# Block attention and two MLPs on one core: y by column blocks at a unit's end, attention by pairs of groups

## The chip, the cores and the metric

One NeuronCore of a Trainium2 chip runs the whole program. The metric is the device time of one execution in microseconds; the lower the better. TensorE (PE) does the matrix products and the transposes, VectorE (DVE) and ScalarE (ACT) the elementwise work and the copies out of PSUM, GpSimd (POOL) elementwise work in SBUF only, and SyncE (SP) issues all DMAs.

## The reference, cut to what matters

```python
B, H, S, D = 2, 8, 768, 64;  block, window = 32, 16
k_sum = k.reshape(B, H, S // block, block, D).max(axis=3)
v_sum = v.reshape(B, H, S // block, block, D).mean(axis=3)
scores_l = q @ k.T / sqrt(D)        # kept where |i - j| < window
scores_s = q @ k_sum.T / sqrt(D) + log(block)
a = softmax(concat(masked scores_l, scores_s))
x = (a @ concat(v, v_sum)) -> rows are tokens: [1536, 512]
y = ((x @ w_a) * (x @ w_b)) @ w_out        # d_ff 1536
h = y @ w_in;  g = maximum(0.01 * h, h)    # d_ff 2048
out = g @ w_out2                           # [1536, 512]
```

All inputs are float32. The weights come in as 64-bit floats, seen as pairs of int32.

## The kernel before, in words

**Tokens and units.** The 1536 tokens are three blocks `c` of T = 512. In the first MLP the 12 slices `f` of 128 columns of `w_a` and `w_b` are taken in runs `s` of M1 = 4; one (s, c) is called a unit here, and there are nine. In the second MLP the 16 slices `f` are taken in runs of M2 = 8. A product of the MLPs is split into a high and a low part on both sides and costs three matmuls (`mm3`), so `x @ w_a` for one slice is 12 matmuls of 128x512. These are all on line 550: 864 for a and b, 432 for y, 576 and 576 in the second MLP, 2448 in all.

**First MLP.** For each slice the kernel writes out the product with `w_a` (bank "a"), the product with `w_b` (bank "b"), and then `y_acc` of the slice before: 12 matmuls that add to four PSUM banks c0 to c3, one for each 128 columns of y. At the unit's last slice the four banks are gathered into SBUF (`gather`). `b_out` multiplies a and b, and `parts` splits the result, in tiles of the pool "g" with two buffers.

**Weights.** A weight piece (512 KB) is loaded by `stage`, and `convert` makes float32 of it in seven steps: VectorE on lines 316, 324, 329, 335, 341 and 349, ScalarE on 320 and 346. The steps wait in the list `bg`. `tick` takes some from it at every `interleave` (three each), and `weights` takes whatever is still missing when a product wants its piece. Converted pieces live in W_EARLY = 15 slots, and in W_LATE = 9 more once the memory of the attention is given back (`att.close`).

**Attention.** A group is two heads by 256 tokens (`GT`), in four windows of 64; there are 24 groups, eight for each token block. `k_prep` transposes k and takes the block maxima, which line 455 copies beside each window. `q_prep` transposes q and writes it as a block-diagonal matrix `qbd` with four ScalarE copies, so that `scores` is four matmuls with the full 128x128 array (line 488; the trace counts two for each). VectorE adds the mask and takes the minimum (line 501), ScalarE takes the exponential (505), `normal` divides (513 and 514 on VectorE, the multiplication on GpSimd, line 515), `p_transpose` (523) and `pv` (534) follow; before `pv`, `put_sums` copies the block means beside the values (182, VectorE). The operations get positions, four to a group, and are written out in that order. Attention's PSUM banks are t0, t1, c2 and c3 during the first token block, and t0 and t1 after it.

**Order.** The first block's attention is written out first, with the products of slices 0 and 1 of block 0 (`early`). The attention of block c + 1 is spread over the products of unit (0, c), and what is left is written out at the unit's end. Instructions are then put in order by a list scheduler with a timeline of its own, by priority in the order written; an engine runs its instructions in the order that results.

Of the kernel before, what the change touches and what calls it, by code (L numbers as in the profile page):

```python
# [16 lines left out]
ALU = mybir.AluOpType  # L17
# [4 lines left out]
def kernel(  # L22
# [45 lines left out]
    W_EARLY, W_LATE = 15, 9  # L68
# [6 lines left out]
    acc_p = ctx.enter_context(tc.tile_pool(name="acc", bufs=2 * NE))  # L75
# [11 lines left out]
    at_banks = ["t0", "t1", "c2", "c3"]  # L87
# [9 lines left out]
    groups = []  # L97
    for c in range(NC):
        here = [divmod(c * GC + i, NGB) for i in range(GC)]
        if here[0][0] == here[-1][0]:  # L100
            groups.append([(b, hp, g) for hp in range(NP) for b, g in here])
        else:
            groups.append([(b, hp, g) for b, g in here for hp in range(NP)])
# [3 lines left out]
        keep.tile([P, NW + 1, SC], F32, tag=f"kts{i}", name=f"kts{i}") for i in range(NP)  # L107
    ]
    ks_t = [keep.tile([P, NB], F32, tag=f"ks{i}", name=f"ks{i}") for i in range(NP)]
    vw_t = [keep.tile([P, 2, G, D], F32, tag=f"vw{i}", name=f"vw{i}") for i in range(2)]  # L110
    qbd_t = [keep.tile([P, G, P], F32, tag=f"qbd{i}", name=f"qbd{i}") for i in range(2)]
# [7 lines left out]
    pace = {"micro": 0.0, "bg": 3}  # L119
# [10 lines left out]
    def load_q(b, hp, g):  # L130
        t = q_p.tile([P, 2, GT // P, D], F32, tag="q", name="q")
        nc.sync.dma_start(
            out=t,
            in_=q[b, 2 * hp : 2 * hp + 2, g * GT : (g + 1) * GT].rearrange(
                "c (p n) d -> p c n d", p=P
            ),
        )
        q_t[b, hp, g] = t
# [12 lines left out]
    def load_vw(b, hp, g):  # L151

        t = vw_t[cnt["load"] % 2]
        cnt["load"] += 1
# [15 lines left out]
        w0, w1 = int(g == 0), G - int(g == NGB - 1)  # L170
        if w0:
            rows(WIN, W, 0, 1)
        rows(0, W, w0, G)
        if w1 == G:
            rows(W, KL, 0, G)
        else:
            rows(W, W + WIN, 0, G)
            rows(W + WIN, KL, 0, w1)
        vw_of[b, hp, g] = t

    def put_sums(b, hp, g):
        nc.vector.tensor_copy(  # L182
            out=vw_of[b, hp, g][W : W + NB],
            in_=vs_t[b, 2 * hp // HV][:, 2 * hp % HV : 2 * hp % HV + 2, :]
            .unsqueeze(2)
            .to_broadcast([NB, 2, G, D]),
        )

    LOAD, SIDE, PRODUCT = range(3)
    PV = 9  # L190

    def attention_ops():

        ops = []
        seen = set()
        for i, x in enumerate(sum(groups, [])):
            b, hp, g = x
            n = 4 * i

            def add(at, kind, f, *args):  # L200
                ops.append((n + at, kind, lambda: f(*args), i))

            vi, r = divmod(2 * hp, HV)
            if (b, hp) not in seen:
                seen.add((b, hp))
                add(-11, LOAD, load_k, b, hp)
                for j in range(NGB):
                    add(j - 9, PRODUCT, k_prep, b, hp, j)
                if r == 0:
                    add(-1, LOAD, load_vb, b, vi)  # L210
                    add(-1, SIDE, v_sums, b, vi)
                    add(5, PRODUCT, v_place, b, vi)
# [9 lines left out]
        return ops  # L222

# [3 lines left out]
    for t in kts_t:  # L227
        nc.vector.memset(t[:, 0, 0:WIN], 0.0)
        nc.vector.memset(t[:, NW, WIN:KP], 0.0)
        nc.vector.memset(t[:, 0:NW, W + NB :], 0.0)  # L230
    for t in qbd_t:
        nc.vector.memset(t, 0.0)
# [29 lines left out]
    slices1 = [(s * M1 + i, c) for s in range(NF1 // M1) for c in range(NC) for i in range(M1)]  # L262
    slices2 = [(s * M2 + i, c) for s in range(NF2 // M2) for c in range(NC) for i in range(M2)]
    uses = [("a", 0), ("b", 0), ("a", 1), ("b", 1), ("a", 2), ("o", 0), ("b", 2), ("o", 1)]
    behind = ("o", 2)
    for f, c in slices1[3:]:
        uses += [("a", f), ("b", f), behind]
        behind = ("o", f)
    for f, c in slices2:
        uses += [("i", f), behind]  # L270
        behind = ("p", f)
    uses.append(behind)
# [87 lines left out]
    def tick(n):  # L360
        for _ in range(n):
            if not bg and may_convert():
                convert()
            if bg:
                bg.pop(0)()
# [3 lines left out]
    def weights(key):  # L369
# [3 lines left out]
        while key not in w_of:  # L373
            if not bg:
                convert()
            bg.pop(0)()
        w, home = w_of[key]
        if last_use[key] == i:
            room[home] += 1
        return w  # L380

# [54 lines left out]
    def k_prep(b, hp, g):  # L436
        k2 = k_t[b, hp]
        kts = kts_t[hp]
        ps = at_bank()
        for i in range(GT // P):  # L440
# [3 lines left out]
        src = ps[:, :GT].rearrange("p (w o) -> p w o", w=G)  # L444
        w0 = g * G
        nc.scalar.copy(out=kts[:, w0 : w0 + G, WIN:W], in_=src[:, :, 0 : W - WIN])
        nc.scalar.copy(out=kts[:, w0 + 1 : w0 + G + 1, 0:WIN], in_=src[:, :, W - WIN :])
        nc.vector.tensor_reduce(
            out=ks_t[hp][:, g * GT // BLK : (g + 1) * GT // BLK],
            in_=ps[:, :GT].rearrange("p (n j) -> p n j", j=BLK),  # L450
# [3 lines left out]
        if g == NGB - 1:  # L454
            nc.vector.tensor_copy(
# [6 lines left out]
    def q_prep(b, hp, g):  # L462
        q2 = q_t.pop((b, hp, g))
        i = cnt["q"] % 2
        cnt["q"] += 1
        qbd = qbd_t[i]
        ps = at_bank()
        for c in range(2):
            nc.tensor.transpose(
                ps[:, c * P : (c + 1) * P], q2[:, c].rearrange("p n d -> p (n d)"), ident  # L470
            )
        sc = -1.0 / math.sqrt(D)
        for c in range(2):

            dst = qbd[c * D : (c + 1) * D, :, c * W : (c + 1) * W].rearrange(
                "p w (o j) -> p w o j", j=2
            )
            src = ps[:, c * P : (c + 1) * P].rearrange("p (w o) -> p w o", w=G)
            nc.scalar.activation(out=dst[:, :, :, 0], in_=src[0:D], func=AF.Copy, scale=sc)
            nc.scalar.activation(out=dst[:, :, :, 1], in_=src[D:], func=AF.Copy, scale=sc)  # L480
        st["qk", b, hp, g] = qbd

    def scores(b, hp, g):
        qbd = st.pop(("qk", b, hp, g))
        kts = kts_t[hp].rearrange("p w o -> p (w o)")
        ps = at_bank().rearrange("p (g k) -> p g k", g=G)
        for w in range(G):
            nc.tensor.matmul(  # L488
                out=ps[:, w, :],
                lhsT=qbd[:, w, :],  # L490
                rhs=kts[:, (g * G + w) * SC : (g * G + w) * SC + P],
                start=True, stop=True,
            )
# [15 lines left out]
        st["pm", b, hp, g] = pm, sm  # L509

    def normal(b, hp, g):
        pm, sm = st["pm", b, hp, g]
# [6 lines left out]
    def p_transpose(b, hp, g):  # L519
        pm, _ = st.pop(("pm", b, hp, g))  # L520
# [3 lines left out]
        pt = at_p.tile([P, G, P], F32, tag="pt", name="pt", bufs=1)  # L524
        nc.scalar.copy(out=pt, in_=ps)
        st["pt", b, hp, g] = pt

    def pv(b, hp, g):
        pt = st.pop(("pt", b, hp, g))
        vw = vw_of.pop((b, hp, g))  # L530
        ps = at_bank()
        for w in range(G):
            for c in range(2):
                nc.tensor.matmul(  # L534
                    out=ps[c * D : (c + 1) * D, w * W : (w + 1) * W],
                    lhsT=vw[:, c, w, :],
                    rhs=pt[:, w, c * W : (c + 1) * W],
                    start=True, stop=True,
                )
        c, t0 = divmod(b * S + g * GT, T)  # L540
        x = x_tile(c, hp)[:, :, t0 : t0 + GT]
        nc.scalar.copy(out=x[:, 0], in_=ps[:, :GT])  # L542
        nc.vector.tensor_tensor(
            out=x[:, 1], in0=ps[:, :GT], in1=x[:, 0].bitcast(F32), op=ALU.subtract
        )
# [22 lines left out]
    def parts(src):  # L568
        t = g_p.tile([P, 2, T], F32R, tag="gs", name="gs")
# [25 lines left out]
    n_first = len(groups[0])  # L595
    per = n_first // NP
    end = 4 * (n_first - 1) + PV
    ops = attention_ops()
    for kt in range(NP):
        ops.append((4 * (per * kt + per - 1) + PV + 5, PRODUCT, lambda kt=kt: early(kt), 0))  # L600
# [5 lines left out]
    for o in ops:  # L606
        if o[0] <= end or o[3] < n_first:
            o[2]()
            if o[1] == PRODUCT and o[0] > 0:
                tick(int(o[0] > PV))  # L610
# [3 lines left out]
    at_banks[2:] = []  # L614
# [11 lines left out]
    acc_tags = [f"c{e}" for e in range(NE)]  # L626
    turn = {"a": ["a"], "b": ["b"], "i": ["a", "b"]}
# [42 lines left out]
    acc = []  # L670

    def y_acc(f, c, gs):
        s, i = divmod(f, M1)
        w = weights(("o", f))
        if i == 0:
# [128 lines left out]
```

## Time and profile before

| | |
|---|---|
| three runs | 689.55, 690.77, 696.64 us, median 690.77 |
| the profiled execution | 693.21 us, span of its instructions 691.4 us |
| mean granted TensorE clock | 0.968 of full speed |
| busy in the span | PE 650.4, DVE 421.7, ACT 293.3, POOL 50.7 us |
| DMA | 53.43 MB, mean 77 GB/s |

The span runs from the first instruction to the last; 1.8 us of the profiled execution lie around it. Busy time of PE is modelled and counts a cold clock as busy; the granted clock of a stretch is given as a share of 2.4 GHz, which is 0.5 at the lower level.

### The profile page before, as it was taken

How to read it: one execution, taken by the hardware profiler on the slowest of the kernel's cores; microseconds unless marked ns; L12 is line 12 of the kernel's file. 1: busy time of each engine (PE TensorE's matmuls, PEld its weight loads, DVE VectorE, ACT ScalarE, POOL GpSimd, SP SyncE). 2: the span in 40 equal slices, each digit the busy share in tenths (PEclk: the TensorE clock that was granted, in tenths of full speed). 3: DMA queues.
4: the chain of work that ended last, by engine and by line, in shares of the span. 5: the costliest groups of instructions: out<-in, count | busy, mean ns of one | idle time of the engine just before them, and what ended most of it. 6: DMA issues, size and time to landing. Idle time of an engine off the chain costs nothing.

```text
span 691.4 us, 9270 instructions
## 1 busy us (share of the span) xinstructions
PE 650.4 (94%) x3248; PEld 533.8 (77%) x3248; DVE 421.7 (61%) x978; ACT 293.3 (42%) x717; POOL 50.7 (7%) x79
## 2 busy tenths in 40 slices
PE   5697895999989999999999999999999999999997
PEld 4575784778768888888888888888888888888886
DVE  4999999443329999679924299943239432322423
ACT  6786566574545544244412255522235332222221
POOL 7324200110110000000000000000000000000000
PEclk9898997699989999999999999999999999999999
DMA  7976356220103444314410024210002000010101
GB/s 170 268 212 182 96 151 173 49 66 20 26 19 123 126 153 136 104 62 127 147 32 0 1 91 145 70 61 1 0 1 92 0 1 0 15 48 0 62 0 62
DMA packets 66862, 53.43 MB, mean 77 GB/s; under 512 B 34304, under 2 KB 60928, under 8 KB 66816
## 3 DMA queue, kind: packets, MB, share of 16 engines
q1 hardware_dynamic: 66816, 52.84, 25.6%
q8 instruction: 26, 0.43, 0.2%
q14 instruction: 20, 0.16, 0.1%
HBM read 49.68 MB, written 3.15 MB: 76 GB/s over the span
## 4 chain that ended last, share of the span: by engine, by line
PE 85%; DVE 8%; DMA 2%; SPq 2%; ACT 1%; issue 1%; DVEq 0%
PE ps_c L550 33%; PE ps_t L550 21%; PE ps_a L550 13%; PE ps_b L550 13%; PE ps_t L488 3%; DVE pm L501 1%; PE ps_t L534 1%; DMA vb<-in_v_dram 1%; DVE wc L335 1%; PE ps_t L523 1%; SPq L168 1%; ACT pm L505 1%; DVE vw L182 1%; DMA wst<-in_moe_w_a_dram 1%; DVE wc L324 1%
## 5 line engine op out<-in xcount | busy, mean ns | idle before, releaser
L550 PE MATMUL ps_c<-wsp,gs 128*128 128x512 f32 x576 | 139.6, 389 | 0.0
L550 PEld LDWEIGHTS ps_c<-wsp,gs 128*128 128x128 f32 x576 | 108.1, 188 | 22.5
L550 PE MATMUL ps_c<-gs,wsp 128*128 128x512 f32 x432 | 106.8, 392 | 0.0
L550 PEld LDWEIGHTS ps_c<-gs,wsp 128*128 128x128 f32 x432 | 80.3, 188 | 16.4
L550 PE MATMUL ps_t<-x,wsp 128*128 128x512 f32 x336 | 80.1, 394 | 0.0
L550 PEld LDWEIGHTS ps_t<-x,wsp 128*128 128x128 f32 x336 | 63.7, 190 | 13.4
L550 PE MATMUL ps_t<-ys,wsp 128*128 128x512 f32 x288 | 72.1, 389 | 0.0
L550 PE MATMUL ps_a<-x,wsp 128*128 128x512 f32 x252 | 69.7, 408 | 0.4 <-ACT x L542 0.2
L550 PE MATMUL ps_b<-x,wsp 128*128 128x512 f32 x252 | 66.5, 397 | 0.0
L550 PEld LDWEIGHTS ps_t<-ys,wsp 128*128 128x128 f32 x288 | 54.1, 188 | 11.2
L320 ACT ACTIVATE wc<-wst 128x512 f32<-128x512 f32 x68 | 46.0, 678 | 37.8 <-DVE wsp L349 37.2
L759 DVE SCALAR_TENSOR_TENSOR h<-h,ps_t 128x512 f32<-128x512 f32 x24 | 16.5, 686 | 67.6 <-ACT h L758 67.6
L550 PEld LDWEIGHTS ps_a<-x,wsp 128*128 128x128 f32 x252 | 47.3, 193 | 10.9 <-ACT x L542 1.7
L550 PEld LDWEIGHTS ps_b<-x,wsp 128*128 128x128 f32 x252 | 47.9, 191 | 9.5
L346 ACT CAST wsp<-wc 128x512 fp32r<-128x512 f32 x68 | 42.2, 622 | 29.4 <-DVE wc L341 27.6
L349 DVE TENSOR_TENSOR wsp<-wc,wsp 128x512 fp32r<-128x512 f32 x68 | 47.5, 699 | 10.5 <-ACT wsp L346 10.4
L335 DVE SCALAR_TENSOR_TENSOR wc<-wst,wc 128x512 int32<-128x512 int32 x68 | 48.9, 720 | 0.4
L341 DVE CUSTOM_DVE_ANT_0 wc<-wc,wr 128x1024 uint16<-128x1024 uint16 x68 | 48.5, 714 | 0.5
L505 ACT ACTIVATE pm<-pm,nb 128x128 f32<-128x128 f32 x96 | 37.7, 395 | 25.2 <-DVE nb L501 25.1
L571 DVE TENSOR_TENSOR gs<-h,gs 128x512 fp32r<-128x512 f32 x48 | 33.2, 691 | 24.7 <-ACT gs L570 24.5
L758 ACT COPY h<-ps_t 128x512 f32<-128x512 f32 x24 | 14.1, 587 | 72.4 <-PE ps_t L550 72.4
L570 ACT CAST gs<-h 128x512 fp32r<-128x512 f32 x48 | 29.8, 621 | 32.5 <-DVE h L759 29.4
(112 smaller groups left out, 800.9 us busy)
## 6 DMA issues: line engine op xcount, KB each, us to landing
wst<-in_moe_w_out_dram SPq DMA_DIRECT2D x28, 512.0 KB, 3.2
wst<-in_moe_w_in_dram SPq DMA_DIRECT2D x16, 512.0 KB, 3.7
wst<-in_moe_w_a_dram SPq DMA_DIRECT2D x12, 512.0 KB, 4.0
wst<-in_moe_w_b_dram SPq DMA_DIRECT2D x12, 512.0 KB, 3.9
k<-in_k_dram SPq DMA_DIRECT2D x16, 192.0 KB, 3.3
q<-in_q_dram SPq DMA_DIRECT2D x24, 128.0 KB, 2.8
vb<-in_v_dram SPq DMA_DIRECT2D x8, 384.0 KB, 5.5
out_dram<-acc SPq DMA_DIRECT2D x12, 256.0 KB, 2.1
```

The costliest lines, as they stand in the source:

```text
L320: nc.scalar.activation(out=t["c"].bitcast(F32), in_=hi_w.bitcast(F32), func=AF.Abs)
L335: nc.vector.scalar_tensor_tensor(out=t["c"], in0=hi_w, scalar=-0x40000000, in1=t["c"], op0=ALU.bitwise_and, op1=ALU.bitwise_or,)
L341: nc.vector.tensor_tensor(out=t["c"], in0=t["c"], in1=t["r"], op=ALU.add)
L346: nc.scalar.copy(out=t["w"][:, 0], in_=t["c"].bitcast(F32))
L349: nc.vector.tensor_tensor(out=t["w"][:, 1], in0=t["c"].bitcast(F32), in1=t["w"][:, 0].bitcast(F32), op=ALU.subtract,)
L488: nc.tensor.matmul(out=ps[:, w, :], lhsT=qbd[:, w, :], rhs=kts[:, (g * G + w) * SC : (g * G + w) * SC + P], start=True, stop=True,)
L505: nc.scalar.activation(out=pm[:, w, :], in_=pm[:, w, :], func=AF.Exp, scale=-1.0, bias=nb[:, w : w + 1], accum_out=sm[:, w : w + 1],)
L550: nc.tensor.matmul(out=ps, lhsT=w(a), rhs=x(b), start=first and j == 0, stop=last and j == 2)
L570: nc.scalar.copy(out=t[:, 0], in_=src)
L571: nc.vector.tensor_tensor(out=t[:, 1], in0=src, in1=t[:, 0].bitcast(F32), op=ALU.subtract)
L758: nc.scalar.copy(out=h, in_=ps)
L759: nc.vector.scalar_tensor_tensor(out=h, in0=h, scalar=0.01, in1=ps, op0=ALU.mult, op1=ALU.max)
```

## The change

1. **y at a unit's end.** A unit now writes out the a and b products of all four slices, and then `y_products`: two column blocks at a time, first slices 0 to 2 of both, then slice 3 of each, whose bank is gathered at once. y uses two banks, c0 and c1, in units (0, 0) and (0, 1) up to its y, and four after that. `gs` gets four buffers; the four pieces of `w_out` of a unit stay until its end. W_EARLY becomes 14 and W_LATE 8, and the late slots open before y of unit (0, 1).
2. **Attention by pairs.** q, values, the transposes of q and the product with the values are handled for two groups at once. The block-diagonal matrix goes: `scores` does each window as two products of 64 rows by 64 columns, one per head, and q is written by one ScalarE copy of 128x512 for two groups. k is prepared in two parts, not three. Attention keeps four banks of its own, t0 to t3, for its whole life.
3. **Engines.** VectorE does the multiplication of `normal`; GpSimd does `put_sums` and the copy of the block maxima.
4. **Conversions.** While the first block's attention is written out, five weights are converted, two steps per product. Each VectorE step of a conversion is ordered behind the last mask instruction (line 501) written before it (`issue_after`). The pace is four steps in unit (0, 0), one in (0, 1), three in (0, 2) and 1.3 from then on.

```diff
-    W_EARLY, W_LATE = 15, 9
+    W_EARLY, W_LATE = 14, 8
-    acc_p = ctx.enter_context(tc.tile_pool(name="acc", bufs=2 * NE))
+    acc_p = ctx.enter_context(tc.tile_pool(name="acc", bufs=NE))
-    at_banks = ["t0", "t1", "c2", "c3"]
+    at_banks = ["t0", "t1", "t2", "t3"]
...
-            add(-7, LOAD, load_q, *x)
-            add(-3, PRODUCT, q_prep, *x)
-            add(0, PRODUCT, scores, *x)
-            add(1, SIDE, normal, *x)
-            add(5, LOAD, load_vw, *x)
-            add(7, SIDE, put_sums, *x)
-            add(8, PRODUCT, p_transpose, *x)
-            add(PV, PRODUCT, pv, *x)
+            add(-14, LOAD, load_q, i, p)
+            add(-6, PRODUCT, q_prep, i, p)
+            for j in range(2):
+                add(4 * j, PRODUCT, scores, i, p, j)
+                add(4 * j + 3, SIDE, normal, i, j)
+                add(4 * j + 8, PRODUCT, p_transpose, i, j)
+            add(1, LOAD, load_vw, i, p)
+            add(9, SIDE, put_sums, i, p)
+            add(PV, PRODUCT, pv, i, p)
...
+    def step():
+        if bg:
+            with tc.issue_after(pace["after"].ins) if pace["after"] is not None else nullcontext():
                 bg.pop(0)()
...
         if g + n == NGB:
-            nc.vector.tensor_copy(
+            nc.gpsimd.tensor_copy(
...
         for w in range(G):
-            nc.tensor.matmul(
-                out=ps[:, w, :],
-                lhsT=qbd[:, w, :],
-                rhs=kts[:, (g * G + w) * SC : (g * G + w) * SC + P],
-                start=True, stop=True,
-            )
+            for c in range(2):
+                h = slice(c * D, (c + 1) * D)
+                nc.tensor.matmul(
+                    out=ps[h, w, :],
+                    lhsT=qt[h, w * W : (w + 1) * W],
+                    rhs=kts[h, (g * G + w) * SC : (g * G + w) * SC + P],
+                    start=True, stop=True,
+                )
...
-            nc.vector.tensor_tensor_reduce(
+            pace["after"] = nc.vector.tensor_tensor_reduce(
...
-        nc.gpsimd.tensor_tensor(
+        nc.vector.tensor_tensor(
             out=pm, in0=pm, in1=sm.unsqueeze(2).to_broadcast([P, G, P]), op=ALU.mult
...
-    at_banks[2:] = []
...
+    def y_products(s, c, gs):
+        ws = [weights(("o", s * M1 + i)) for i in range(M1)]
+        def add(ps, e, i):
+            mm3(
+                ps,
+                lambda j: ws[i][:, j, e * P : (e + 1) * P],
+                lambda j: gs[i][:, j],
+                i == 0, i == M1 - 1,
+            )
+        for e in range(0, NE, 2):
+            ps = [product_bank("y") for _ in range(2)]
+            for i0, i1 in ((0, M1 - 1), (M1 - 1, M1)):
+                for j in range(2):
+                    for i in range(i0, i1):
+                        add(ps[j], e + j, i)
+                    if i1 == M1:
+                        if e + j == NE - 1:
+                            free()
+                        y = gather("y", c, e + j, ps[j], s, NF1 // M1)
+                        if s == NF1 // M1 - 1:
+                            y_parts(c, e + j, y)
+                    interleave()
...
+    for s, c in units:
+        todo = range(len(gs), M1)
+        pace["bg"] = {(0, 0): 4, (0, 1): 1, (0, 2): 3}.get((s, c), 1.3)
...
+        for i in todo:
+            pa = first_product(("a", s * M1 + i), xt, c)
+            g = a_out(pa)
+            interleave()
+            pb = first_product(("b", s * M1 + i), xt, c)
+            gs.append(b_out(pb, g))
+            interleave()
+        drain()
+        if (s, c) == (0, NC - 2):
             att.close()
             late["wsp"] = ctx.enter_context(tc.tile_pool(name="wsp2", bufs=W_LATE))
...
+            turn.update({"a": ["a", "t0"], "b": ["b", "t1"], "y": ["c0", "c1", "t2", "t3"]})
+            turn["i"] = ["a", "b", "t0", "t1"]
+        y_products(s, c, gs)
+        gs = []
```

## Rows read from the trace of the kernel before

**Rows 1.** Page, part 2: VectorE's busy tenths in 40 slices of the span.

```profile
DVE  4999999443329999679924299943239432322423
```

**Rows 2.** Busy time by windows: PE, PEld, DVE, ACT, POOL, granted clock, DMA share, GB/s.

```profile
0.00:20.00 20.00, 11.85 (x55) 10.26 (x56) 9.72 (x48) 12.21 (x47) 13.31 (x48) 1.00 0.75 189
20.00:120.00 100.00, 77.25 (x531) 61.00 (x532) 96.86 (x275) 69.95 (x233) 25.80 (x20) 0.88 0.64 178
120.00:148.40 28.40, 25.60 (x200) 20.06 (x197) 13.18 (x59) 18.22 (x71) 5.34 (x5) 0.77 0.22 54
148.40:204.60 56.20, 52.51 (x342) 42.84 (x341) 19.33 (x83) 26.46 (x92) 6.24 (x6) 0.94 0.12 29
204.60:686.00 481.40, 481.40 (x2125) 398.56 (x2125) 280.14 (x511) 166.48 (x276) 0.00 (x0) 1.00 0.18 57
686.00:691.40 5.40, 1.78 (x8) 1.12 (x6) 2.50 (x4) 0.00 (x0) 0.00 (x0) 1.00 0.52 194
```

**Rows 3.** The same windows, line 550 alone: PE and PEld busy, clock, DMA.

```profile
20.00:120.00 100.00, 40.83 (x144) 26.72 (x144) 0.88 0.64 178
120.00:148.40 28.40, 9.02 (x25) 4.68 (x25) 0.77 0.22 54
148.40:204.60 56.20, 39.12 (x150) 28.20 (x151) 0.94 0.12 29
204.60:686.00 481.40, 481.40 (x2125) 398.56 (x2125) 1.00 0.18 57
```

**Rows 4.** Line 349, the last step of a conversion, by windows: DVE busy.

```profile
20.00:120.00 100.00, 11.20 (x15) 0.88 0.64 178
```

**Rows 5.** Groups by line and shape: busy us and mean ns, then idle before.

```profile
L335 DVE SCALAR_TENSOR_TENSOR wc<-wst,wc 128x512 int32<-128x512 int32 x68 | 48.9, 720 | 0.4
L341 DVE CUSTOM_DVE_ANT_0 wc<-wc,wr 128x1024 uint16<-128x1024 uint16 x68 | 48.5, 714 | 0.5
L349 DVE TENSOR_TENSOR wsp<-wc,wsp 128x512 fp32r<-128x512 f32 x68 | 47.5, 699 | 10.5 <-ACT wsp L346 10.4
L329 DVE TENSOR_SCALAR wc<-wc 128x512 int32<-128x512 int32 x68 | 29.8, 439 | 0.2
L324 DVE TENSOR_SCALAR wc<-wc 128x512 f32<-128x512 f32 x68 | 29.2, 430 | 1.1 <-ACT wc L320 0.9
L316 DVE TENSOR_SCALAR wr<-wst 128x512 int32<-128x512 uint32 x68 | 28.6, 420 | 2.9 <-DMA wst<-in_moe_w_a_dram 1.3 <-DMA wst<-in_moe_w_in_dram 1.1 <-DMA wst<-in_moe_w_out_dram 0.3
L515 POOL TENSOR_TENSOR pm<-pm,sm 128x512 f32<-128x512 f32 x24 | 26.3, 1096 | 141.1 <-DVE sm L514 89.1 <-PE ps_t L523 11.4 <-ACT g L578 10.3
L182 DVE COPY vw<-vs 24x512 f32<-24x512 f32 x24 | 12.4, 529 | 1.0 <-ACT vs L430 0.2 <-PE ps_c L534 0.2
L455 DVE COPY kts<-ks 128x288 f32<-128x288 f32 x8 | 4.6, 572 | 0.1
```

**Rows 6.** Line 513 by itself: ns min/median/max.

```profile
L513 DVE TENSOR_SCALAR sm<-sm x24: 148/168/1225, 15.6 to 195.5; 128x4 f32<-128x4 f32 x24
```

**Rows 7.** The chain of waits, 60 to 210 us: start us, us, what.

```profile
148.42 2.95 PE ps_a L550 x12
...
158.44 0.89 PE ps_t L488 x8
159.33 0.62 PE ps_t L534 x16
...
164.72 0.22 PE ps_t L469 x2
...
165.86 0.44 PE ps_t L523 x4
...
196.37 1.52 SPq L168
197.94 1.64 DMA vw<-in_v_dram
```

**Rows 8.** Who waited for whom: us in total, times, longest us.

```profile
DVE wsp L349 <- ACT wsp L346: 10.4, 5, 4.5
```

More of the change, by code (lines that the diff above doesn't have):

```diff
@@ L1 @@
 import math
-from contextlib import ExitStack
+from contextlib import ExitStack, nullcontext
 import numpy as np
@@ L93, in at_bank @@
         return bank(at_banks[cnt["at"] % len(at_banks)])
-    groups = []
+    pairs = []
     for c in range(NC):
@@ L118 @@
     bg, vb_done = [], [None]
-    pace = {"micro": 0.0, "bg": 3}
+    pace = {"micro": 0.0, "bg": 3, "after": None}
     q_t, k_t, vb_t, vw_of = {}, {}, {}, {}
@@ L128, in load_k, with load_q @@
         k_t[b, hp] = t
[L130 to L136, printed above, removed]
-        )
-        q_t[b, hp, g] = t
+    def load_q(i, p):
+        t = q_p.tile([P, 2 * GT // P, 2, D], F32, tag="q", name="q")
+        for j, b, hp, g, n in runs(p):
+            for c in range(2):
+                nc.sync.dma_start(
+                    out=t[:, j * GT // P : (j + n) * GT // P, c, :],
+                    in_=q[b, 2 * hp + c, g * GT : (g + n) * GT].rearrange(
+                        "(n p) d -> p n d", p=P
+                    ),
+                )
+        q_t[i] = t
     def load_vb(b, i):
@@ L375, in weights, with free @@
                 convert()
-            bg.pop(0)()
+            step()
         w, home = w_of[key]
         if last_use[key] == i:
-            room[home] += 1
-        return w
+            spent.append(home)
+            if key[0] != "o":
+                free()
+        return w
+    spent = []
+    def free():
+        while spent:
+            room[spent.pop()] += 1
     xt = {}
@@ L523, in p_transpose, with pv @@
             nc.tensor.transpose(ps[:, w, :], pm[:, w, :], ident)
-        pt = at_p.tile([P, G, P], F32, tag="pt", name="pt", bufs=1)
+        pt = at_p.tile([P, G, P], F32, tag="pt", name="pt")
         nc.scalar.copy(out=pt, in_=ps)
[L526 to L530, printed above, removed]
+        st["pt", i, j] = pt
+    def pv(i, p):
+        vw = vw_of.pop(i)
         ps = at_bank()
[L532 to L545, printed above, removed]
+        for j in range(2):
+            pt = st.pop(("pt", i, j))
+            for w in range(G):
+                for c in range(2):
+                    nc.tensor.matmul(
+                        out=ps[c * D : (c + 1) * D, j * GT + w * W : j * GT + (w + 1) * W],
+                        lhsT=vw[:, c, j * G + w, :],
+                        rhs=pt[:, w, c * W : (c + 1) * W],
+                        start=True, stop=True,
+                    )
+        for j, b, hp, g, n in runs(p):
+            c, t0 = divmod(b * S + g * GT, T)
+            src = ps[:, j * GT : (j + n) * GT]
+            x = x_tile(c, hp)[:, :, t0 : t0 + n * GT]
+            nc.scalar.copy(out=x[:, 0], in_=src)
+            nc.vector.tensor_tensor(
+                out=x[:, 1], in0=src, in1=x[:, 0].bitcast(F32), op=ALU.subtract
+            )
     def mm3(ps, w, x, first, last):
@@ L593, in early @@
             kt_mm(ps, w, xt[0, kt], kt)
-    n_first = len(groups[0])
-    per = n_first // NP
-    end = 4 * (n_first - 1) + PV
+    N_FIRST = 5
+    n_first = len(pairs[0])
+    end = PER * (n_first - 1) + PV
     ops = attention_ops()
     for kt in range(NP):
-        ops.append((4 * (per * kt + per - 1) + PV + 5, PRODUCT, lambda kt=kt: early(kt), 0))
+        ops.append((PER * kt + PV + 5, PRODUCT, lambda kt=kt: early(kt), 0))
     firsts = ((("a", 0), "a"), (("b", 0), "b"), (("a", 1), "c0"), (("b", 1), "c1"))
@@ L623 @@
     assert not held
-    acc_tags = [f"c{e}" for e in range(NE)]
-    turn = {"a": ["a"], "b": ["b"], "i": ["a", "b"]}
+    turn = {"a": ["a"], "b": ["b"], "y": ["c0", "c1"]}
     def product_bank(nm):
@@ L698, with drain @@
+    def drain():
+        while micro:
+            micro.pop(0)[1]()
+    for s, c in units:
+        todo = range(len(gs), M1)
+        pace["bg"] = {(0, 0): 4, (0, 1): 1, (0, 2): 3}.get((s, c), 1.3)
+        if s == 0 and c + 1 < NC:
+            last = PER * (sum(len(p) for p in pairs[: c + 2]) - 1) + PV
             micro += [o for o in later_ops if o[0] <= last]
             later_ops = later_ops[len(micro) :]
-            pace["micro"] = len(micro) / (per_slice * (M1 - (2 if c == 0 else 0)) - 2.0)
+            pace["micro"] = len(micro) / (4 * len(todo) - 1.0)
@@ L701 @@
             cnt["credit"] = 0.0
-        if s == 0 and i == 0 and c == NC - 1:
-            while micro:
-                micro.pop(0)[1]()
+        for i in todo:
[7 more added lines that the diff above has]
+        if (s, c) == (0, NC - 2):
             att.close()
             late["wsp"] = ctx.enter_context(tc.tile_pool(name="wsp2", bufs=W_LATE))
-            late["y", NC - 1] = late["o", NC - 1] = ctx.enter_context(
-                tc.tile_pool(name="acc2", bufs=NE)
-            )
+            acc2 = ctx.enter_context(tc.tile_pool(name="acc2", bufs=2 * NE))
+            late.update({(stage, c): acc2 for stage in "yo" for c in range(1, NC)})
@@ L763 @@
         interleave()
-        if prev is None:
-            y_acc(*pend)
-        else:
+        if prev is not None:
             o_acc(*prev)
-        interleave()
+            interleave()
         prev = f, c, hs
```

229 lines of the change are left out of this document (96 added, 133 removed).

## The prediction

> **What bounds the kernel now.** I read the windows first. From 204.6 us to 686 us TensorE is busy for the whole stretch at full clock with nothing but line 550, 2125 matmuls in 481.40 us, 0.2265 us each [rows 2, 3]. That rate is the floor of this work: the 2448 matmuls of the MLPs need 554.5 us, and the change touches neither their number nor their shape. So whatever is to be won lies before 204.6 us, where only 319 of them run (144 + 25 + 150) and 72.3 us would do for them [rows 3].
>
> What holds up those 204.6 us differs by stretch. From 20 to 120 us VectorE is busy for 96.86 of 100 us [rows 1, 2]; TensorE's clock is 0.88 there, so part of it runs at the lower level, and line 550 gets 144 matmuls, 33 us' worth. Fifteen conversions fall into it [rows 4]. From 120 to 148.4 us no engine is full: VectorE 13.18 of 28.4 us, 25 matmuls, clock 0.77 [rows 2, 3]: this is the latency of the attention's chain, which had been queued behind conversions. From 148.4 to 204.6 us the products and the attention of the third block share TensorE well until about 184 us, then the last groups stand alone; the chain of waits even goes through SP issuing the values' loads and one of those loads, 1.52 and 1.64 us [rows 7]. A floor for this last stretch is 150 matmuls or 34.0 us and, for about five groups, 2.17 us each (0.89 + 0.62 + 0.22 + 0.44) [rows 7], 45 us in all against 56.2: 11 us stand empty.
>
> **Part by part.** I follow when the dense stretch can begin. After the change this needs (A) VectorE's work up to y of unit (0, 0): attention of 16 groups and 12 converted pieces; (B) y of unit (0, 0), the a and b products of (0, 1) with the attention of block 2, and y of (0, 1); then everything else is dense (C), and the tail follows (D).
>
> (A) VectorE is busy 9.72 + 96.86 + 13.18 = 119.8 us up to 148.4 us [rows 2], by when the 16 groups are done. A conversion costs it 720 + 714 + 699 + 439 + 430 + 420 ns = 3.42 us [rows 5]; twelve in place of fifteen save 10.3 us. `put_sums` goes to GpSimd: 16 groups by 529 ns, 8.5 us; the copies of block maxima too, 8 by 572 ns, 4.6 us [rows 5]. The multiplication comes in: no row has it on VectorE, and the nearest is line 349, also two SBUF tensors of 128x512, 699 ns, so 16 of them cost 11.2 us. That leaves 107.6 us. The old figure also holds two conversions that had begun and about two groups of block 2; for these I take off up to 8 us, an estimate from the same rows, so the work is 100 to 108 us, and I take 104. VectorE was idle 10.3 us of the first 20 [rows 2], while k, q and the mask come in, and this stays; from 20 to 120 us it idled 3.1 us, and I allow 2. So (A) ends at 116 us, with 110 (work of 100, no further idling) and 131 (see the second rival) as ends.
>
> (B) y of a unit is 48 matmuls, 10.9 us, twice; a and b of four slices are 96, 21.8 us; eight groups at 2.17 us are 17.4 us. Sum 61.0 us. Stalls: the last pair's chain has y of (0, 1) to hide behind, and pairs issue their loads of values in half the number of DMAs in blocks 0 and 2, so the 1.52 us of SP goes with them; with four banks the transposes and scores no longer wait for the evacuation two steps before. I allow 6 us of the 11 that stand empty now; ends 0 and 17 (the 11 and 6 more).
>
> (C) Nine units have 144 matmuls, two of them are through, so 2160 by 0.2265 us, 489.3 us. Slots fall from 24 to 22 and the pace to 1.3 steps, so I counted, by the order in which steps and products are written, how far conversions run ahead: 25 pieces are done when unit (1, 0), which needs 24, begins, 50 when the second MLP begins, and after unit (0, 0) no product has to force its piece. VectorE is busy 280.14 of 481.40 us there [rows 2], enough room. What is late next is y itself: the split of slice 3 is wanted 18 matmuls (4.1 us) after product b ends, against a product or two more before. VectorE's multiplication and subtraction at about 0.7 us each (as line 349 [rows 5]) and a ScalarE cast between them that is no longer than these take 2.1 us; I put it at nothing, and at 2 us per unit, nine times, if conversion steps stand ahead of it.
>
> (D) The last matmul ends 1.78 us into the last window, so 3.6 us of writing out remain [rows 2].
>
> Small terms. The tiled scores do 16 quarter-size pieces where eight full ones took 0.89 us, 0.11 each [rows 7]. Two heads side by side would halve the time, sixteen in a row would double it: between -0.4 and +0.9 us a group, -3 to +7 us on the eight groups of (B); `pv`, whose sixteen pieces are half as wide, needs 0.62 us for them, so I take nothing. GpSimd loses 24 by 1096 ns and gains copies of 24 partitions and 8 of 128x288, which no row shows on it; by line 515 at most 2 ns an element, 1024 elements a pair is between nothing and 2.2 us a pair, off the path, since `pv` comes four positions later. ScalarE loses the four copies of `qbd` and is nowhere the bound (69.95 of 100 us [rows 2]). Rows of q now come in half-size runs; with a DMA share of 0.64 [rows 2] and loads written two pairs ahead I cost this at nothing, at 3 us if the first pairs wait.
>
> The sum is 116 + 61.0 + 6 + 489.3 + 3.6 = 675.9 us of span. With 1.8 us around it this is 677.7 us against the profiled 693.21; the median of the runs lies 2.4 us below that execution, so I forecast **675 us**.
>
> **Two rules weighed.** Line 513 works on 128x4 elements and takes 148 ns at best and 1225 at worst [rows 6]; the excess is about the 1096 ns of one multiplication on GpSimd [rows 5]. The Trainium skill, SBUF — State Buffer, "Who interferes with whom", says that a VectorE instruction with two SBUF inputs or in a two-port mode and a GpSimd instruction that reads SBUF lock each other out, the second waiting for all of the first; by that rule the sums that GpSimd now copies would hold up conversions in their turn, and the relief from line 515 would be partly given back, which leaves the sum as it is.
>
> The pieces of `pv` already stand between full-size matmuls, and the twelve matmuls after such a burst took 2.95 us where twelve take 2.72 at the dense rate [rows 7, 3]. The Trainium skill, TensorEngine Tiling (Array Packing), "Key Properties", says that a change of tiling mode drains TensorE, and this speaks against quarter-size scores; by the row a change costs at most 0.23 us, so two more for each of eight groups would add 3.7 us and give 679.
>
> **Rivals.** *VectorE starves in the first part* (chance 0.2). Only five conversions are let into the first block's attention, 17 us, with about half of the other 63 us; if TensorE at its lower clock stretches that part to some 65 us, VectorE idles 15 us more, and the seven conversions left are paid afterwards, in full, before y of (0, 0). For it: the clock of 0.88 and 77.25 us of TensorE busy from 20 to 120 us [rows 2]. Against it: the next block's preparation is written in early. (A) ends at 131: 690 us.
>
> *More comes back* (0.15). The lower end of (A), 108 with less waiting for GpSimd, and no stalls in (B), since the scheduler fills gaps with products: 661 us.
>
> *The ordering makes conversions serial* (0.12, the one on the other side). A conversion step may not pass the last mask step before it, which waits for scores on TensorE, which may stand behind a product that waits for the conversion. Then two conversions no longer overlap. VectorE's last step has waited for ScalarE's cast 2.1 us a time, 10.4 us in five waits [rows 8]; paid at each of twelve conversions it is 25 us: 700 us. It makes the kernel slower by over 1% from 1.9 us a conversion on. Against it: attention steps lie between and can fill.
>
> *Scores double* (0.1): 7 us on (B): 682 us.
>
> *The order does not change* (0.08): the scheduler had its reasons and places conversions ahead as before; VectorE's smaller work stays, (B) has its 17 us of stalls: 686 us.
>
> **How the numbers follow.** The forecast has 0.35. About 1% (7 us) is what a measurement of this kernel can tell from no change: faster is below 683.9, slower above 697.7. Faster has the forecast, 661 and 682, 0.60; within 1% has 690 and 686, 0.28; slower 0.12. The range, 659 to 696, takes in all but the serial case, and the ends of (A) and (B).
>
> **What would show it.** Right: line 550 dense from about 185 us on, with 288 matmuls done before it; line 349 counted 12 to 14 times before y of (0, 0), which starts at 110 to 120 us; VectorE full up to there; no idle TensorE between a unit's b and its y. Wrong: gaps of VectorE before line 501 during conversions (serial), idling of VectorE before 60 us (starved), gaps on line 550 after 200 us (the y cover or the slots), or bursts of line 488's successor of 1.8 us at full clock (scores double).

## The result, and the profile after

The changed kernel takes **661.88 us** (median of four runs, 660.72 to 663.29) against 692.91 us before (four runs, 689.55 to 696.64): a ratio of 0.9552, interval 0.9491 to 0.9612. The forecast of 675 us had the sign, and its range holds the time; 661 us is what the rival *more comes back* gave, though in part by another way (below). The profiled execution took 661.53 us, 659.8 of it span, 31.6 us less span than before.

Page, parts 1 and 2:

```profile
PE 636.2 (96%) x3440; PEld 519.3 (79%) x3440; DVE 418.1 (63%) x952; ACT 270.8 (41%) x609; POOL 48.5 (7%) x79
...
DVE  3999889955999962699623869732279532422323
...
PEclk9898999999999999999999999999999999999999
```

The slices are 16.5 us long. VectorE is again nearly full, here up to about 132 us (eight slices); in [rows 1] it was to 120 us. What is new is that TensorE is full beside it from 97 us on. The granted clock, 0.97 on the mean before, is 0.99. Windows, columns as in [rows 2]; first all instructions:

```profile
0.00:20.00 20.00, 10.69 (x79) 8.52 (x81) 9.20 (x42) 8.99 (x33) 12.96 (x49) 0.99 0.88 223
20.00:97.00 77.00, 66.44 (x682) 51.93 (x678) 70.49 (x232) 55.71 (x189) 29.27 (x28) 0.94 0.73 175
97.00:168.00 71.00, 70.88 (x531) 55.00 (x532) 53.79 (x167) 40.54 (x114) 6.26 (x3) 1.00 0.31 89
168.00:656.00 488.00, 488.00 (x2154) 403.85 (x2152) 283.70 (x514) 165.61 (x274) 0.00 (x0) 1.00 0.18 58
```

From 97 us on TensorE is busy 70.88 of 71 us, then 488.00 of 488, at full clock. Before, that began at 204.6 us [rows 2]. Next, line 583 alone (the MLP matmul that was line 550), split where its 288th matmul is done:

```profile
0.00:97.00 97.00, 25.18 (x85) 15.32 (x85) 0.95 0.76 185
97.00:136.30 39.30, 30.14 (x113) 20.05 (x113) 1.00 0.43 123
136.30:166.40 30.10, 22.65 (x92) 16.50 (x92) 1.00 0.17 49
166.40:659.80 493.40, 489.75 (x2161) 405.18 (x2159) 1.00 0.19 59
```

The first three rows count 290, two of them across a border. What comes after 166.4 us takes 493.4 us; the terms (C) and (D) were 492.9. So all of the gain over the forecast lies ahead of 166.4 us, and that part the forecast had end at 183 us.

What VectorE had done by 97 us is seen on two lines, each alone by windows with VectorE's busy time: line 531 (the mask, eight instructions a group) first, then line 365 (the last step of a conversion; line 349 before):

```profile
0.00:97.00 97.00, 15.09 (x128) 0.95 0.76 185
```

```profile
0.00:97.00 97.00, 5.23 (x7) 0.95 0.76 185
97.00:168.00 71.00, 6.07 (x9) 1.00 0.31 89
```

All 16 groups are masked, with only seven pieces converted. Before, the same 97 us held twelve groups (96 masks, line 501) and eleven of the fifteen conversions of [rows 4] (line 349):

```profile
0.00:97.00 97.00, 11.54 (x96) 0.91 0.68 185
```

```profile
0.00:97.00 97.00, 8.51 (x11) 0.91 0.68 185
```

What TensorE does while the other conversions run is on the timeline of the changed kernel (start us, us, line, tile, count):

```profile
107.82 0.60 PE L553 MATMUL ps_t<-ident,pm 128*128 128x128 f32 x4
108.17 1.17 PE L583 MATMUL ps_c<-gs,wsp 128*128 128x512 f32 x4
109.18 0.62 PE L583 MATMUL ps_a<-x,wsp 128*128 128x512 f32 x2
109.64 0.62 PE L583 MATMUL ps_b<-x,wsp 128*128 128x512 f32 x2
...
110.64 1.09 PE L518 MATMUL ps_t<-kts,qt 64*64 64x128 f32 x16
...
130.57 5.73 PE L583 MATMUL ps_c<-gs,wsp 128*128 128x512 f32 x24
```

y of unit (0, 0), on `ps_c`, is spread from 108 to 136 us. Between its pieces stand the a and b products of unit (0, 1), whose weights were converted for (0, 0) already, and the attention of block 2. The scheduler put them there; as the program is written, y comes first.

### The profile page after: what moved, and what is told of

The parts are those of the page before. It is cut to its first block, busy times and chain, and to the rows that moved or that the text cites. A ratio compares the mean times of both kernels' runs of the same rounds, so it can differ in the third digit from the quotient of the medians.

```text
span 659.8 us, 9339 instructions
## 1 busy us (share of the span) xinstructions
PE 636.2 (96%) x3440; PEld 519.3 (79%) x3440; DVE 418.1 (63%) x952; ACT 270.8 (41%) x609; POOL 48.5 (7%) x79
## 4 chain that ended last, share of the span: by engine, by line
PE 88%; DVE 6%; POOL 2%; DMA 1%; issue 1%; SPq 1%; ACT 0%; POOLq 0%; DVEq 0%
PE ps_t L583 38%; PE ps_c L583 18%; PE ps_a L583 14%; PE ps_b L583 13%; PE ps_t L518 2%; PE ps_t L565 1%; DVE pm L545 1%; PE ps_t L553 1%; DMA vb<-in_v_dram 1%; DVE pm L531 1%; POOL vb L425 1%; PE ps_t L472 1%; SPq L182 1%; DVE sm L543 0%; DVE acc L688 0%
## 5 line engine op out<-in xcount | busy, mean ns | idle before, releaser
L583 PE MATMUL ps_t<-x,wsp 128*128 128x512 f32 x336 | 78.4, 389 | 0.0
L583 PE MATMUL ps_c<-wsp,gs 128*128 128x512 f32 x288 | 75.9, 389 | 0.0
L583 PE MATMUL ps_t<-wsp,gs 128*128 128x512 f32 x288 | 74.7, 389 | 0.0
L583 PE MATMUL ps_a<-x,wsp 128*128 128x512 f32 x252 | 66.0, 399 | 1.8 <-ACT x L575 1.0
L583 PEld LDWEIGHTS ps_t<-wsp,gs 128*128 128x128 f32 x288 | 54.0, 188 | 11.3
L583 PEld LDWEIGHTS ps_c<-wsp,gs 128*128 128x128 f32 x288 | 54.1, 188 | 11.2
L583 PE MATMUL ps_c<-gs,wsp 128*128 128x512 f32 x240 | 61.0, 394 | 0.0
L583 PEld LDWEIGHTS ps_a<-x,wsp 128*128 128x128 f32 x252 | 46.8, 190 | 11.9 <-ACT x L575 1.3
L790 DVE SCALAR_TENSOR_TENSOR h<-h,ps_t 128x512 f32<-128x512 f32 x24 | 16.5, 686 | 60.3 <-ACT h L789 60.3
L583 PEld LDWEIGHTS ps_c<-gs,wsp 128*128 128x128 f32 x240 | 44.4, 188 | 9.6 <-DVE wr L332 0.2
L583 PE MATMUL ps_t<-gs,wsp 128*128 128x512 f32 x192 | 47.5, 389 | 0.0
L351 DVE SCALAR_TENSOR_TENSOR wc<-wst,wc 128x512 int32<-128x512 int32 x68 | 46.6, 688 | 0.3
```

The source lines that it names most:

```text
L351: nc.vector.scalar_tensor_tensor(out=t["c"], in0=hi_w, scalar=-0x40000000, in1=t["c"], op0=ALU.bitwise_and, op1=ALU.bitwise_or,)
L583: nc.tensor.matmul(out=ps, lhsT=w(a), rhs=x(b), start=first and j == 0, stop=last and j == 2)
L790: nc.vector.scalar_tensor_tensor(out=h, in0=h, scalar=0.01, in1=ps, op0=ALU.mult, op1=ALU.max)
```

## The experiments

The *before* kernels start from the kernel before, the others from the changed one. Ratios are to the kernel before, run beside it on the same chip, with a 95% interval.

**The order edge.** Conversion steps without the wait on the last mask step:

```diff
-            with tc.issue_after(pace["after"].ins) if pace["after"] is not None else nullcontext():
-                bg.pop(0)()
+            bg.pop(0)()
```

> The changed kernel, with the conversions' VectorE steps no longer ordered behind the last mask step. Theory (order): VectorE took attention first only because of this edge, so conversions again stand before masks, the 16 groups end some 10 us later than at 97 us, and the time is 670 to 680 us. Rival (amount): the later, sparser conversions (five in the first part, paced after) already keep VectorE free for attention, and the time stays at 660 to 665 us.

665.21 us, 0.9583 (0.9551 to 0.9614). By 97 us 13 groups are masked (105 mask instructions) instead of 16, and still the time is only some 2 to 3 us more, not separated from the changed kernel by the intervals.

**The multiplication on GpSimd.** `nc.vector.tensor_tensor` of `normal` back to `nc.gpsimd.tensor_tensor`.

> The changed kernel, with the multiplication of the softmax back on GpSimd, the sums' copies staying there too. Theory (load): VectorE gets rid of 16 multiplications of 860 ns before 97 us, 14 us, but GpSimd's 1.04 us and the longer chain take their place and its other work blocks VectorE, so 660 to 666 us. Rival (port): the multiplication on GpSimd was a main cost of the kernel before through waits of VectorE, and the time rises to 670 us or more. Third: VectorE's load is what bounds the first 97 us, and the time falls by 5 us or more, to 657 us or less.

668.48 us, 0.9624 (0.9590 to 0.9658), between the two, and not separated from the changed kernel by the intervals. It gains nothing at least, although VectorE has less to do, and its timeline shows a wait that stands against that:

```profile
90.00 1.11 PE L553 MATMUL ps_t<-ident,pm 128*128 128x128 f32 x4 [2.77 <-POOL pm L545]
```

The transposes of p wait for GpSimd. From 80 to 100 us VectorE is busy 7.54 of 20 us and TensorE's clock falls to 0.75, so some of that stretch runs at 1.2 GHz. There the chain is waited for, not VectorE.

**The copies of sums on VectorE.** `nc.gpsimd.tensor_copy` back to `nc.vector.tensor_copy` in `put_sums` and for the block maxima.

> The changed kernel, with the copies of block means and block maxima back on VectorE. Theory (load): 12 to 13 us more on VectorE before 97 us; as VectorE was busy 79.7 of 97 us, about two thirds of it show: 668 to 674 us. Rival (chain): the first 97 us are bound by waits from engine to engine, VectorE has 17 us of room there and GpSimd's copies took 0.7 to 1.6 us each: 659 to 664 us.

671.71 us, 0.9667 (0.9624 to 0.9710): 8 us more, where the theory put it; 14 groups masked by 97 us (112). That it comes from the load alone isn't shown: VectorE's copies take 8.4 us by then, but from 20 to 97 us it is busy 67.65 us, less than the 70.49 of the changed kernel, and idles more.

**y before the products of the next unit.** Every a and b product of unit (0, 1) waits for the last matmul of y of (0, 0):

```diff
-            nc.tensor.matmul(
+            with tc.issue_after(hold["pe"].ins) if hold["pe"] is not None else nullcontext():
+                hold["last"] = nc.tensor.matmul(
```

> The changed kernel, with every matmul of the a and b products of unit (0, 1) ordered behind the last matmul of y of unit (0, 0) on TensorE, which is the order that the forecast assumed. Theory (fill): TensorE is full from 97 us on because these products run while the last four or five conversions for y are made; without them y waits for 4.6 conversions of 3.4 us: 672 to 680 us, close to the forecast. Rival (no fill): y of (0, 0) would be ready almost as early, since VectorE then has nothing else: 660 to 666 us.

667.06 us, 0.9612 (0.9573 to 0.9651), nearer to the rival, and the interval still overlaps that of the changed kernel. Block 2's attention still ran ahead: 96 pieces of its scores, six groups, stand between 97 and 131.6 us, where y ends.

**All of the next unit behind y.** The same wait around the whole of unit (0, 1), block 2's attention included. This is the order in which the forecast added its terms, but for two groups of block 2, whose scores are written out in unit (0, 0).

> The changed kernel, with everything that unit (0, 1) has on TensorE, block 2's attention too, ordered behind the last matmul of y of unit (0, 0): the serial order that the forecast took for (A) and (B). With its products alone held the time was 667 us. Theory (serial was the error): y waits for the twelfth conversion with nothing to fill, and the time is 670 to 680 us, at the forecast of 675. Rival: VectorE then does the last conversions at once, y begins some 12 us after 97 us, and the time stays at 664 to 668 us.

672.33 us, 0.9697 (0.9646 to 0.9749): 10 us more, as expected of the serial order. All instructions by windows, then the timeline of TensorE:

```profile
97.00:127.40 30.40, 23.71 (x157) 17.14 (x152) 28.19 (x72) 17.19 (x44) 4.40 (x4) 0.89 0.57 156
127.40:177.70 50.30, 50.30 (x409) 39.56 (x408) 26.96 (x95) 24.63 (x76) 2.84 (x2) 1.00 0.14 38
177.70:671.10 493.40, 489.79 (x2161) 405.18 (x2159) 286.28 (x519) 166.44 (x276) 0.00 (x0) 1.00 0.19 59
```

```profile
110.49 5.67 PE L585 MATMUL ps_c<-gs,wsp 128*128 128x512 f32 x12 [4.60 <-ACT wsp L362]
```

y now waits for conversions (4.60 us before this group of its matmuls), VectorE is full (28.19 of 30.4 us), and TensorE is empty for 6.7 of the 30.4 us. The 493.4 us behind are those of the changed kernel to the tenth.

**The engines alone, on before.** The multiplication to VectorE, the copies of sums to GpSimd.

> The kernel before, with only the change of engines: the multiplication on VectorE, the copies of means and maxima on GpSimd. By the two runs that undid these in the changed kernel (5 and 8 us), theory (engines): 8 to 15 us off, a ratio of 0.978 to 0.988 to the kernel before. Rival (only together): in the kernel before conversions fill VectorE from 20 to 120 us whatever else it has, so the copies' 13 us less and the multiplications' 11 us more change nothing: a ratio of 0.995 to 1.005.

688.19 us (nine runs), 0.9943 (0.9913 to 0.9973): some 4 us, just outside the rival's range and far from the theory's. VectorE stays as full as it was, since conversions take what was freed. All engines first, then line 349 and line 550, each alone:

```profile
20.00:97.00 77.00, 63.60 (x438) 51.34 (x437) 75.58 (x219) 57.68 (x184) 25.25 (x21) 0.91 0.70 190
```

```profile
0.00:97.00 97.00, 10.69 (x13) 0.91 0.71 191
```

```profile
97.00:100.00 3.00, 2.11 (x8) 1.42 (x8) 1.00 0.58 200
100.00:120.00 20.00, 0.00 (x0) 0.00 (x0) 0.55 0.46 128
```

Thirteen pieces are converted by 97 us instead of eleven, and no more groups are masked (96 masks). The 144 products of unit (0, 0) are used up at 100 us, and for 20 us none follows, at a granted clock of 0.55.

**The three VectorE parts together, on before.** The engines, the order edge and five conversions in block 0's attention; groups, banks and y as before.

> The kernel before, with the change of engines, the conversions ordered behind the mask steps, and five conversions in the first part; groups, banks and y as before. Theory (VectorE first): these three free VectorE for attention and bring most of the 31 us: a ratio of 0.965 to 0.975. Rival (banks and y): without attention's own four banks and with y after each slice, whose pieces are wanted from the second product on, conversions can't be put off, and no more than 10 us come: 0.985 to 1.0.

692.38 us (ten runs), 0.9986 (0.9961 to 1.0012): nothing. All engines, in the stretch that decides:

```profile
100.00:120.00 20.00, 14.24 (x96) 10.64 (x98) 10.39 (x32) 11.33 (x43) 7.00 (x7) 0.64 0.31 82
```

VectorE is free for half of it now, and TensorE is empty for 5.8 of 20 us and runs partly at the lower clock. Only two matmuls of the MLPs fall into it. Here it is not that the products of unit (0, 0) are used up: by 97 us 96 of them are done, which is what eight pieces allow. Line 349 shows that the ninth piece is not finished before 120 us, with VectorE half free:

```profile
0.00:97.00 97.00, 7.15 (x8) 0.88 0.65 167
97.00:120.00 23.00, 0.00 (x0) 0.62 0.28 73
```

Its steps are ordered behind masks, and VectorE idles up to 2.2 us at a time for the scores that the next masks need. The conversions that were put off are now what TensorE lacks, as the rival had it.

**Pairs as well, on before.** Adds the attention by pairs to the last; y after each slice and the attention's banks stay (`t0`, `t1`, and `c2`, `c3` until the MLP takes them).

> The changed kernel's attention by pairs, engines, five early conversions and order of conversions, but y after each slice on four banks and attention's banks as in the kernel before (t0, t1, c2, c3, then t0 and t1). It stands between the three parts alone (ratio 0.9986) and the changed kernel with the old banks (0.976). Theory (reserve): y kept for the unit's end is what lets TensorE work while block 1's attention ends, so pairs alone bring little: a ratio of 0.985 to 1.0. Rival (pairs): fewer banks and copies for two groups shorten the attention itself, and most of the 2.3% is theirs: 0.973 to 0.983.

681.06 us, 0.9833 (0.9766 to 0.9901), between theory and rival.

**The banks of before.** The changed kernel with two banks for attention after the first part and four for y from the start:

```diff
+    at_banks[2:] = []
-    turn = {"a": ["a"], "b": ["b"], "y": ["c0", "c1"]}
+    turn = {"a": ["a"], "b": ["b"], "y": ["c0", "c1", "t2", "t3"]}
```

> The changed kernel, with attention on the two banks t0 and t1 after the first part, as in the kernel before, and y on four. Theory (banks): with two banks each transpose and score waits for the evacuation of the one two steps before; the work of blocks 1 and 2 loses the cover, TensorE shows gaps up to 160 us: 668 to 680 us. Rival: VectorE sets the pace to 97 us and products fill the rest, so 660 to 665 us.

676.84 us, 0.9761 (0.9718 to 0.9804): 14 us more, the most of any part that was undone by itself (y's banks and attention's were moved together). VectorE is less busy from 20 to 97 us (61.56 against 70.49 us), and TensorE waits, step for step:

```profile
90.46 1.93 PE L518 MATMUL ps_t<-kts,qt 64*64 64x128 f32 x16 [1.02 <-ACT qt L504]
97.45 0.65 PE L553 MATMUL ps_t<-ident,pm 128*128 128x128 f32 x4 [1.00 <-DVE x L576]
98.84 0.66 PE L500 MATMUL ps_t<-ident,q 128*128 128x128 f32 x4 [0.73 <-ACT pt L555]
100.95 1.09 PE L518 MATMUL ps_t<-kts,qt 64*64 64x128 f32 x16 [1.02 <-ACT qt L504]
```

**More conversions early.** `N_FIRST = 5` set to 12.

> The changed kernel, with twelve conversions in place of five allowed while the first block's attention is written out. Theory (putting off): that conversions come late is where the time beyond the forecast came from; seven of 3.4 us before the 16 groups are done move these from 97 to some 115 us, of which the earlier y gives part back: 670 to 678 us. Rival: the step order keeps them behind attention anyway: 660 to 664 us.

666.58 us, 0.9595 (0.9544 to 0.9647): between the two, some 3 us more, with intervals that overlap; 13 groups masked by 97 us (104).

**Full-array scores.** q block-diagonal as before, eight products a group for sixteen quarter-size ones; two ScalarE copies a pair for one, weight slots 13 and 9.

> The changed kernel, with scores as four products of the full 128x128 array a group, from a block-diagonal tile that two ScalarE copies fill for a pair (one weight slot moved from early to late to make room). Theory (no matter): the sixteen pieces take 1.02 us a group where the eight took 0.89, 1 us on the eight groups of block 2, and ScalarE's copies are hidden: 659 to 664 us. Rival (tiles pay): the pieces keep TensorE and its clock busier in the first 97 us or save a chain step: 666 us or more.

660.92 us, 0.9540 (0.9487 to 0.9594): the same as the changed kernel. Groups of this kernel, then of the changed one:

```profile
L525 PE MATMUL ps_t<-kts,qbd 128*128 128x128 f32 x192 | 27.3, 288 | 2.4 <-POOL negm_last L277 1.2 <-ACT pt L562 0.8 <-DVE nb L538 0.3
```

```profile
L518 PE MATMUL ps_t<-kts,qt 64*64 64x128 f32 x384 | 29.7, 296 | 2.8 <-ACT pt L555 1.5 <-POOL negm_last L272 1.2
```

Twice the number of products, 29.7 us for 27.3.

**The multiplication on ScalarE.** Four `activation(Copy, scale=sm[:, w])` a group.

> The changed kernel, with the softmax's multiplication on ScalarE, four windows a group, in place of VectorE's one instruction, which took 963 ns on the mean before 97 us because GpSimd held it up. Theory (VectorE bounds the first 97 us): 14 us less on an engine that is busy 79.7 of 97 us there, ScalarE going from 65 to 84: 652 to 658 us, better than the changed kernel. Rival (the chain bounds it): ScalarE's queue, with the exponentials in it, becomes the slower step: 662 to 670 us.

666.89 us, 0.9634 (0.9577 to 0.9692). All engines by window:

```profile
20.00:97.00 77.00, 67.05 (x662) 52.05 (x662) 60.00 (x216) 67.64 (x236) 23.71 (x26) 0.93 0.71 172
```

VectorE has 10.5 us less to do in this stretch than in the changed kernel (60.00 against 70.49), and the kernel gains nothing, as the rival had it. ScalarE has 11.9 us more (67.64 against 55.71), so the run shows that this exchange doesn't pay, not that VectorE's load is without effect. No version tried is measurably faster than the changed kernel.

## Why the prediction was right, and where it was off

**(C) and (D)** held: 493.4 us against 492.9, TensorE 488.00 of 488 us. So the y cover, the slots and the pace cost nothing, as taken.

**The step that failed is in (A):** the wait for the twelfth converted piece, and y of (0, 0) behind it, were put ahead of all the rest of (B). Run x10 sets that order and tests the terms one by one. In it y of (0, 0) ends at 127.4 us; the forecast said 116 + 10.9 = 126.9. From there to the dense stretch it takes 50.3 us; the forecast said 50.1 and 6 of stalls. So the sum comes out for its order, except for the stalls, 5.8 us, which aren't there. The changed kernel reaches the same point at 166.4 instead of 177.7 us. These 11.3 us are what the order is worth (10 us by the ratios): five conversions run under products of (0, 1) and block 2's attention. Together, 11.3 + 5.8 − 0.5 is the 16.6 us by which 183 was too late. The rival *more comes back* had no stalls, because the scheduler fills gaps, and that came true. Its other half, (A) done at 108 us, did not: the twelfth piece is finished at 123.2 us in the changed kernel, and what was filled is the wait for it. So the rival's 661 us is in part luck. The forecast gave it 0.15, since it read the order of the program as the order of the queue.

**Luck in (A).** That x10 meets the forecast to half a microsecond is luck too. Line 365 in x10 has the twelfth piece at 120.4 us, not at 116; all engines up to there:

```profile
119.70 0.69 DVE L365 TENSOR_TENSOR wsp<-wc,wsp 128x512 fp32r<-128x512 f32 x1
```

```profile
0.00:120.40 120.40, 91.93 (x846) 70.54 (x846) 96.26 (x329) 75.76 (x252) 43.64 (x77) 0.90 0.71 176
```

VectorE had 96.3 us of work where the forecast took 104, and idled 24.1 us where it allowed 12. Against the 4.4 us by which this is later, y had begun at 110.5 us, on the pieces that were there. And the scores of two of the eight groups of (B), 2.2 us, ran ahead of y's end.

**VectorE's work** was forecast too high, as x10 shows, although the multiplication was mis-sized the other way. This is the changed kernel up to 97 us:

```profile
L545 DVE TENSOR_TENSOR pm<-pm,sm 128x512 f32<-128x512 f32 x15 | 14.4, 963 | 0.2
L425 POOL TENSOR_TENSOR vb<-vb,vb 96x512 f32<-96x512 f32 x8 | 11.5, 1457 | 11.5 <-DMA vb<-in_v_dram 6.0 <-DMA q<-in_q_dram 5.5
```

Up to 97 us it takes 963 ns and not the 699 of [rows 5], 4 us more on 16 groups; over the whole kernel the mean is 860. The reason is in the timeline of VectorE and GpSimd:

```profile
53.49 3.12 POOL L425 TENSOR_TENSOR vb<-vb,vb 96x512 f32<-96x512 f32 x2 [5.51 <-DMA q<-in_q_dram]
53.73 1.76 DVE L545 TENSOR_TENSOR pm<-pm,sm 128x512 f32<-128x512 f32 x1
55.41 1.23 DVE L543 TENSOR_SCALAR sm<-sm 128x4 f32<-128x4 f32 x1
...
57.78 1.59 POOL L425 TENSOR_TENSOR vb<-vb 96x512 f32<-96x512 f32 x1
58.17 1.75 DVE L545 TENSOR_TENSOR pm<-pm,sm 128x512 f32<-128x512 f32 x1
59.85 0.68 DVE L482 TENSOR_REDUCE ks<-ps_t 128x16 f32<-128x512 f32 x1
...
60.58 0.69 PE L472 MATMUL ps_t<-ident,k 128*128 128x128 f32 x2 [3.91 <-DVE ks L482]
```

Beside GpSimd's adds the multiplication takes 1.75 us instead of 0.69 at its median, and a 128x4 operation 1.23 us. TensorE is empty for 3.91 us while VectorE works off such a multiplication, two steps of a conversion and the maxima of line 482. The relief of VectorE is partly given back to the additions of `v_sums`, which were on GpSimd before as well. There the prediction misread [rows 6]: it put the 1225 ns of line 513 down to a multiplication on GpSimd, but both long ones in the kernel before, at 51.98 and 69.89 us, stand beside these additions (line 396). The first of them:

```profile
50.04 3.13 POOL L396 TENSOR_TENSOR vb<-vb,vb 96x512 f32<-96x512 f32 x2
51.98 1.23 DVE L513 TENSOR_SCALAR sm<-sm 128x4 f32<-128x4 f32 x1
```

Moving the multiplication does not touch this. The rule of the Trainium skill that the prediction weighed (SBUF — State Buffer, "Who interferes with whom") agrees with these rows: the later of the two waits for the whole of the other. When the multiplication of 58.17 us begins, 1.2 us of the add are left, and it takes 1.06 us longer than its median.

**The banks** were only a part of the five of 11 us of stalls that the forecast let go. They measure 14 us: with two banks a transpose or a score waits 0.7 to 1.0 us for the evacuation of the step that had its bank last. That is the largest single part that was undone, and the least worked out in the prediction.

**Alone, the VectorE parts are worth nothing** (0.9986), where the prediction set out from a full VectorE. The ladder of ratios: the three VectorE parts 0.9986; with pairs 0.9833; with y at a unit's end, on the old attention banks, 0.9761; with four banks for attention 0.9552. The parts don't add up: from the changed kernel, the copies of sums are worth 8 us and the multiplication's place some 5 by the ratios, which the intervals don't separate. In the old layout the engines alone free VectorE for more conversions, and unit (0, 0)'s products are gone at 100 us, ahead of block 1's attention; with the other two parts as well, products wait for conversions that were put off. Either way TensorE has an empty stretch at 100 us. Once it has other work at hand, the place of VectorE's work counts, by the 8 us of the copies; load and waits were not told apart there.

**The scores** went as taken: sixteen quarter-size pieces 29.7 us for 27.3 in all 24 groups, 0.1 us a group, within −0.4 to +0.9. The drain that the Trainium skill (TensorEngine Tiling (Array Packing), "Key Properties") gives for a change of mode shows no price in the time: the kernel without quarter-size scores is as fast. The pieces of `pv` are in both kernels, so this tests the scores alone.

**The signs to look for:** VectorE was nearly full up to y (81.0 of 88 us from 20 to 108 us), and there was no gap at the y cover. Two came earlier than said: the dense stretch at 166.4 us and not at about 185, and y at 108 us and not at 110 to 120. Not so "line 349 counted 12 to 14 times before y": eight when y begins. *Starved*, *serial conversions*, *scores double* and *order doesn't change* did not happen; the edge costs nothing (without it the kernel is, if anything, slower). What stays open is how pairs and y at a unit's end divide their gain: their intervals (0.9833 and 0.9761) overlap.

## What to carry to other kernels

An engine that is 97% busy need not be the bound: ask what the others would do if it were free. Three parts that unloaded VectorE gave nothing while TensorE had no product ready to stand in for the attention's latency. Give a chain of small dependent matmuls enough banks, and keep products whose weights are ready for the place where something else must be waited for. When you add up stages, ask for each sum whether the scheduler is bound to its order; one added wait (x10) showed what the order was worth, 11.3 us.

## What was not expected of the hardware

The granted clock fell with TensorE's gaps: with the three VectorE parts on the kernel before, 14.24 busy of 20 us went with 0.64, and with only the engines changed, a stretch without MLP matmuls had 0.55; the changed kernel from 97 us on had 1.00. A stretch with gaps so loses twice, in the gaps and in matmuls at the lower of the two levels (1.2 GHz): two MLP matmuls took 1.20 us in the first of these stretches (at 111 us) and 0.62 us in the changed kernel (at 109 us). A 128x4 operation of VectorE, 164 ns at its median, took 1.23 us while GpSimd added 96x512 tiles; the prediction had weighed this wait, but for another instruction of GpSimd and without a term in its sum.
